# Decayed state on GpSimd, two row-tile homes changed, and wider-spaced weight conversions in a fused attention and expert kernel

## The chip, the cores and the metric

One core of a Trainium2 chip runs the whole program. The metric is device time in microseconds (us). Three runs of the kernel before took 591.41, 592.48 and 594.57 us, so the median is 592.48 us.

## What is computed

The reference has three parts in a row. The first is causal attention with decay: 2 batches, 8 heads, 768 positions, head size 64, and a 64x64 state per head that is decayed and added to from block to block. The second is a dense feed-forward layer on the 1536 tokens that result. The third sends every token to the best of 8 experts.

```python
kv_state = lam_block[None, :, None, None] * kv_state + np.einsum('bhsd,bhse->bhde', kb_dec, vb)
...
h = x @ w_in
g = h * np.tanh(sp)
return (g @ w_out).astype(np.float32)
...
h = np.maximum(x[mask] @ w1[e], 0.0)
out[mask] = gate_w[mask, None] * (h @ w2[e])
```

## The kernel before, in words

**Tiling.** The 1536 tokens are 12 tiles of 128. Attention handles one tile per call of attend (L837), with blocks of 128 positions instead of 64, so six calls make a batch. Three tiles make a chunk of 384 tokens, and there are four chunks. The dense layer has 2048 hidden units in 16 pieces of 128, numbered fc. For a chunk and a piece, mm1 (L791) does twelve matmuls into PSUM and a chain of five ScalarE and five VectorE instructions for the activation. mm2a (L815) does nine matmuls that add the piece to three PSUM accumulators, one per token tile. Every operand is held as a high and a low part, hence three products for each.

**Order of the main loop (L861).** Step i takes one pair (chunk, piece) from a list of 64: chunks 0, 1 and 2 with pieces 0 to 7, then the same chunks with pieces 8 to 15, then chunk 3 with all 16. In a step mm1 works on pair i, and mm2a on pair i-3. There are only three accumulators. After pieces 0 to 7 of a chunk, put_by (L386) copies the three accumulators with ScalarE into row tiles and sends them to memory. Later fetch (L392) loads them back, and route (L410) adds them. So put_by happens in steps 10, 18 and 26 for chunks 0, 1 and 2, and mm2a of the next step needs the accumulators empty. The first fetch stands in step 32. Attention tiles 3 to 11 are done inside steps 0 to 8.

**Weights.** Each of the 32 weight pieces (16 of w_in, 16 of w_out) arrives as 64-bit floats and is converted on the chip. load_wi (L286) and load_wo (L295) take a staging tile (L281), load 512 KB into it on SyncE's queue, and call convert (L269): three ScalarE instructions (L272, L273, L276), two VectorE (L274, L275) and one GpSimd subtraction (L277, shown under the helper's line L102). The staging tile is free again when that subtraction is done. Staging tiles come from a list of tags used in turn. In steps 9 and on the list is `cv, wo14, cv, wo15`, and from the moment that the next conversion is piece 13 of w_in it is `cv, cv`. The tag cv has two buffers; wo14 and wo15 have one each, which hold attention tiles (pms, L137) before, and the converted pieces 14 and 15 of w_out at the end. convert_next (L305) takes the next pieces in order. Half of the 32, those with fc under 8, are converted in the attention steps. In steps from 9 on, L873 asks for 2, 1, 1, 2, 1, 1 and so on.

**Row tiles.** row_tiles (L378) gives put_by, fetch and the last route one cv buffer, which holds two rows of tiles, and the tile xq, which holds the third.

**State.** combine (L193) computes a tile's contribution to the state in PSUM (sp, L203). For the first tile of a batch it is copied (L218). For the next four, VectorE decays the old state and adds sp in one instruction per pair of heads: four instructions of 128x64 (L221). The sixth tile of a batch needs no new state. So there are 32 such instructions. GpSimd in attention scales the keys and the queries (L188, L191, both shown under L102) and does the conversions' subtractions.

**What sets the order on a queue.** Each engine and SyncE's queue runs its instructions in a fixed order. It is made ahead of time, from the place in the program and from when each instruction is reckoned to be ready. So a later conversion can stand ahead of an earlier instruction that is not ready, and a load can stand far ahead of its use.

Of the kernel before, what the change touches and what calls it, by code (L numbers as in the profile page):

```python
# [7 lines left out]
F32 = mybir.dt.float32  # L8
# [5 lines left out]
ALU = mybir.AluOpType  # L14
AX = mybir.AxisListType
P = 128
# [10 lines left out]
FA = 8  # L27
# [4 lines left out]
def tile_decay_attention_mish_moe_top1(  # L32
# [16 lines left out]
    B, H, S, D = q.shape  # L49
    NT, DM = out.shape  # L50
    NE, _, FF = w1.shape
    HP = H // 2
# [13 lines left out]
    def T(shape, dt, tag, bufs=1):  # L66
        return pool.tile(shape, dt, tag=tag, name=tag, bufs=bufs)
# [28 lines left out]
    def PS(shape, tag):  # L96
        return psp.tile(shape, F32, tag=tag, name=tag, bufs=NBUF[tag])

    V, A, G = nc.vector, nc.scalar, nc.gpsimd

    def tt(o, a, b, op, eng=None):
        (eng or V).tensor_tensor(out=o, in0=a, in1=b, op=op)  # L102

    def bc(ap, n):
        return ap.unsqueeze(len(ap.shape)).to_broadcast(list(ap.shape) + [n])
# [32 lines left out]
    sts = T([P, 4, HP, D], F32, "wo13")  # L138
# [8 lines left out]
    def qT(it):  # L147
        return qTs[it // 2 % 2][:, it % 2]
# [44 lines left out]
    def combine(it):  # L193
        b, c = it // CPB, it % CPB
        kd, vt = kd2[:, it % 2], vr2[:, it % 2]
        pm = pms[it % 2]
        qd = qT(it)
        st_old, st_new = sts[:, c % 2], sts[:, (c + 1) % 2]
        if c < CPB - 1:
            sp = PS([P, HP, D], "w" if it < SHARED else "r")  # L200
            for hp in range(HP):
                for r in range(2):
                    nc.tensor.matmul(sp[64 * r:64 * r + 64, hp, :], lhsT=kd[:, 2 * hp + r, :], rhs=vt[:, 2 * hp + r, :],  # L203
                                     start=True, stop=True)
        po = PS([P, HP, P], "a" if it < SHARED else "w")
        for hp in range(HP):
            for r in range(2):
                s = slice(64 * r, 64 * r + 64)
                if c > 0:
                    nc.tensor.matmul(po[s, hp, :], lhsT=st_old[s, hp, :], rhs=qd[s, hp, :], start=(hp == 0), stop=False,  # L210
                                     skip_group_check=True)
        for hp in range(HP):
            for r in range(2):
                s = slice(64 * r, 64 * r + 64)
                nc.tensor.matmul(po[s, hp, :], lhsT=vt[:, 2 * hp + r, :], rhs=pm[:, r, hp, :], start=(c == 0 and hp == 0), stop=True,
                                 skip_group_check=True)
        if c == 0:
            V.tensor_copy(st_new, sp)  # L218
        elif c < CPB - 1:
            for hp in range(HP):  # L220
                V.scalar_tensor_tensor(out=st_new[:, hp], in0=st_old[:, hp], scalar=lc[:, hp:hp + 1], in1=sp[:, hp],  # L221
                                       op0=ALU.mult, op1=ALU.add)
        ck, o = it // CT, (it % CT) * P
        if o == 0:
            xth[ck] = T([P, KC, CW], F32R, f"xth{ck}")
            xtl[ck] = T([P, KC, CW], F32R, f"xtl{ck}")
        A.activation(out=xth[ck][:, :, o:o + P], in_=po, func=AF.Copy)
        tt(xtl[ck][:, :, o:o + P], po, xth[ck][:, :, o:o + P].bitcast(F32), ALU.subtract)
# [31 lines left out]
    lc = tabq[:, :, P - 1]  # L260
# [44 lines left out]
    def convert_next(n, limit=NFC):  # L305
        for _ in range(n):
            ok = [w for w in wq if w[2] < limit]
            if ok:
                wq.remove(ok[0])
                _, kind, f = ok[0]  # L310
                (load_wi if kind == "i" else load_wo)(f)
# [66 lines left out]
    def row_tiles():  # L378
        xa = T([P, 2, DM], F32, "cv", 2)
        xq = T([P, DM], F32, "xq")  # L380
        return [xa[:, 0], xa[:, 1], xq[:, :]]

    def part_rows(c, j):
        return part[(CT * c + j) * P:(CT * c + j + 1) * P, :]

    def put_by(c, acc):  # L386
        rows = row_tiles()
        for j in range(CT):
            A.activation(out=rows[j], in_=acc[j], func=AF.Copy, scale=2.0)  # L389
            nc.sync.dma_start(out=part_rows(c, j), in_=rows[j])  # L390
# [394 lines left out]
    def step():  # L785
        if steps:
            f = steps.pop(0)
            if f is not None:
                f()
# [71 lines left out]
    for i, (c, fc) in enumerate(order):  # L861
        it = CT + i
        if it < NIT:
            if it == NIT - CT:
                stg["tags"] = ["cv", "cv", "wi10"]
            attend(it)
            convert_next(2, FA)
        else:
            if it == NIT:
                stg["tags"] = ["cv", "wo14", "cv", "wo15"]  # L870
            if wq and wq[0][2] >= 13:
                stg["tags"] = ["cv", "cv"]
            convert_next(2 if i < FA + 1 or i % 3 == 0 else 1)  # L873
        mm1(c, fc)
        step()
        if c == NCK - 1:
            early(1, fc)
        if i >= LAG:
            mm2a(*order[i - LAG])
        step()  # L880
# [310 lines left out]
```

## Time and profile before

| | us |
|---|---|
| runs | 591.41, 592.48, 594.57 |
| profiled execution, whole | 593.29 |
| its span, first to last instruction | 591.6 |
| PE busy | 534.8 |
| VectorE busy | 342.3 |
| ScalarE busy | 303.1 |
| GpSimd busy | 114.9 |

The profiled execution is 0.81 us above the median of the runs. 1.7 us of it lie outside the span. Busy time of PE is an upper bound of its work, because matmuls overlap and their ends are modelled. The granted clock of TensorE, 1.00 for 2.4 GHz, tells where the same matmuls ran slower: its other level, 1.2 GHz, is half.

### The profile page before, as it was taken

The page shows a single profiled execution, that of the slowest core. Times are in us where ns is not written, and L with a number is a line of the kernel's source. Part 1 is how long each engine was busy: PE and PEld are TensorE (multiplying, and loading weights), DVE is VectorE, ACT ScalarE, POOL GpSimd, SP SyncE. Part 2 cuts the span into 40 slices and gives each one's busy share as a digit, 9 for nine tenths or more (in the row PEclk, how much of TensorE's full clock was granted, in tenths as well). Part 3 has the DMA queues.
Part 4 walks back from the last instruction along what each step waited for, and adds up shares of the span by engine and source line. Part 5 has one row for each costly group of instructions (what it writes and reads, how often), then busy time and mean ns, then how long its engine had stood idle before and what let it go on. Part 6 is the DMA issues. An engine that isn't in the chain of part 4 may idle for free. (4 is left out here: it accounts for less than half of the span.)

```text
span 591.6 us, 10189 instructions
## 1 busy us (share of the span) xinstructions
PE 534.8 (90%) x3568; PEld 465.9 (79%) x3568; DVE 342.3 (58%) x815; ACT 303.1 (51%) x581; POOL 114.9 (19%) x99
## 2 busy tenths in 40 slices
PE   4899899999879999999999999999889968878990
PEld 2678788888768989899999998898788858667870
DVE  3467898777987765867677699748320233212110
ACT  3257878568888666566565678531221244112110
POOL 1264464422221100000000012001413022030300
PEclk9999999999898999999999999988999998989996
DMA  8669874224343020020030072001696183020300
GB/s 200 154 153 251 204 200 144 81 81 143 107 124 108 18 90 1 0 90 19 0 108 1 27 251 96 2 10 48 202 342 244 38 274 124 10 83 12 93 24 19
DMA packets 67214, 61.76 MB, mean 104 GB/s; under 512 B 42151, under 2 KB 51887, under 8 KB 67120
## 3 DMA queue, kind: packets, MB, share of 16 engines
q1 hardware_dynamic: 64304, 51.70, 29.1%
q0 software_dynamic: 2816, 8.92, 4.9%
q8 instruction: 46, 0.75, 0.6%
q14 instruction: 48, 0.39, 0.2%
HBM read 51.94 MB, written 8.86 MB: 103 GB/s over the span
## 5 line engine op out<-in xcount | busy, mean ns | idle before, releaser
L824 PE MATMUL a<-wo,mg 128*128 128x512 f32 x576 | 149.5, 402 | 5.1 <-ACT xq L389 2.8
L798 PE MATMUL w<-xth,wi 128*128 128x384 f32 x512 | 144.2, 342 | 2.9 <-DVE me L810 2.5
L824 PEld LDWEIGHTS a<-wo,mg 128*128 128x128 f32 x576 | 108.4, 191 | 27.7 <-ACT xq L389 3.8
L798 PEld LDWEIGHTS w<-xth,wi 128*128 128x128 f32 x512 | 93.9, 188 | 7.1 <-DVE me L810 2.9
L576 PE MATMUL w<-wi,wi 128*128 128x256 f32 x576 | 78.1, 295 | 15.3 <-issue 12.0
L576 PEld LDWEIGHTS w<-wi,wi 128*128 128x128 f32 x576 | 74.9, 200 | 18.3 <-issue 13.6
L798 PE MATMUL w<-xtl,wi 128*128 128x384 f32 x256 | 86.3, 337 | 0.0
L580 DVE SCALAR_TENSOR_TENSOR wo<-w,wi 128x256 fp32r<-128x256 f32 x48 | 20.0, 424 | 91.5 <-ACT wi L579 88.3
L566 PE MATMUL a<-wo,wi 128*128 128x512 f32 x192 | 62.8, 409 | 3.7 <-ACTq L1135 2.8
L808 DVE SCALAR_TENSOR_TENSOR me<-me,mg 128x384 f32<-128x384 f32 x64 | 42.2, 659 | 34.7 <-ACT mg L807 34.7
L579 ACT ACTIVATE wi<-w 128x256 fp32r<-128x256 f32 x48 | 18.1, 385 | 66.6 <-PE w L576 65.4
L798 PEld LDWEIGHTS w<-xtl,wi 128*128 128x128 f32 x256 | 48.3, 188 | 1.8
L803 ACT ACTIVATE me<-w 128x384 f32<-128x384 f32 x64 | 31.1, 485 | 30.1 <-PE w L798 29.9
L566 PEld LDWEIGHTS a<-wo,wi 128*128 128x128 f32 x192 | 35.7, 192 | 13.0 <-issue 5.5
L805 ACT ACTIVATE me<-me,one 128x384 f32<-128x384 f32 x64 | 39.2, 612 | 12.6 <-DVE me L804 12.3
L811 ACT ACTIVATE mg<-me 128x384 fp32r<-128x384 f32 x64 | 33.3, 521 | 23.5 <-DVE me L810 23.1
L102 DVE TENSOR_TENSOR mg<-me,mg 128x384 fp32r<-128x384 f32 x64 | 37.5, 586 | 11.9 <-ACT mg L811 11.2
L806 ACT ACTIVATE mr<-me,one 128x384 f32<-128x384 f32 x64 | 39.3, 614 | 1.2
L809 DVE SCALAR_TENSOR_TENSOR me<-me,mg 128x384 f32<-128x384 f32 x64 | 38.3, 599 | 1.0
L566 PE MATMUL a<-wo,wo 128*128 128x512 f32 x96 | 38.5, 402 | 0.0
L810 DVE SCALAR_TENSOR_TENSOR me<-me,w 128x384 f32<-128x384 f32 x64 | 35.2, 550 | 1.2
L807 ACT ACTIVATE mg<-mr 128x384 fp32r<-128x384 f32 x64 | 33.4, 522 | 1.3
(268 smaller groups left out, 699.7 us busy)
## 6 DMA issues: line engine op xcount, KB each, us to landing
xtl<-in_moe_w_dram SPq DMA_DIRECT2D x24, 256.0 KB
cv<-in_moe_w_out_dram SPq DMA_DIRECT2D x11, 512.0 KB
cv<-in_moe_w_in_dram SPq DMA_DIRECT2D x9, 512.0 KB
wi<-in_moe_w_dram SPq DMA_DIRECT2D x8, 512.0 KB
wo<-in_moe_w_dram SPq DMA_DIRECT2D x8, 512.0 KB
wo<-in_k_dram SPq DMA_DIRECT2D x12, 256.0 KB
wi<-in_q_dram SPq DMA_DIRECT2D x12, 256.0 KB
wo<-in_v_dram SPq DMA_DIRECT2D x12, 256.0 KB
```

Source lines behind the costliest of these rows:

```text
L102: (eng or V).tensor_tensor(out=o, in0=a, in1=b, op=op)
L566: nc.tensor.matmul(po, lhsT=a_, rhs=b_, start=(f == 0 and i == 0), stop=(f == FC2 - 1 and i == 2))
L576: nc.tensor.matmul(ph, lhsT=a_, rhs=b_, start=(n == 0), stop=(n == 3 * KC - 1))
L798: nc.tensor.matmul(ph, lhsT=a_, rhs=b_, start=(n == 0), stop=(n == 3 * KC - 1))
L805: A.activation(out=ex, in_=ex, func=AF.Square, bias=one[:, 0:1])
L806: A.activation(out=rr, in_=ex, func=AF.Ln, bias=one[:, 0:1])
L807: A.activation(out=gg[:, 1], in_=rr, func=AF.Exp, scale=-1.0)
L808: V.scalar_tensor_tensor(out=ex, in0=ex, scalar=1.0, in1=gg[:, 1].bitcast(F32), op0=ALU.add, op1=ALU.mult)
L809: V.scalar_tensor_tensor(out=ex, in0=ex, scalar=-2.0, in1=gg[:, 1].bitcast(F32), op0=ALU.add, op1=ALU.mult)
L810: V.scalar_tensor_tensor(out=ex, in0=ex, scalar=0.5, in1=ph, op0=ALU.add, op1=ALU.mult)
L811: A.activation(out=gg[:, 0], in_=ex, func=AF.Copy)
L824: nc.tensor.matmul(accs[c][j], lhsT=a_, rhs=b_, start=(fc in (0, divided_at) and i == 0), stop=(fc in (divided_at - 1, NFC - 1) and i == 2))
```

## The change

Three edits. The state's decay becomes one GpSimd multiplication of 128x256 into a third slice of the state tile, and one VectorE addition of 128x256 takes the place of the four instructions. For chunks 0 and 1, put_by takes its row tiles under the tags wo15 (rows 0 and 1) and wo14 (row 2) instead of cv and xq; chunk 2 and everything later stay with cv and xq. In the main loop the conversions asked for in steps 9 and on become 0, 1, 1, 0, 1, 1 and so on. (The new condition `i <= FA` never holds there, since this branch starts with step 9 and FA is 8.)

```diff
-        st_old, st_new = sts[:, c % 2], sts[:, (c + 1) % 2]
+        st_old, st_new, st_dec = sts[:, c % 2], sts[:, (c + 1) % 2], sts[:, 2]
...
-            for hp in range(HP):
-                V.scalar_tensor_tensor(out=st_new[:, hp], in0=st_old[:, hp], scalar=lc[:, hp:hp + 1], in1=sp[:, hp],
-                                       op0=ALU.mult, op1=ALU.add)
+            tt(st_dec, st_old, bc(lc, D), ALU.mult, G)
+            tt(st_new, sp, st_dec, ALU.add)
...
     def put_by(c, acc):
-        rows = row_tiles()
+        if c < 2:
+            xa = T([P, 2, DM], F32, "wo15")
+            xb = T([P, 2, DM], F32, "wo14")
+            rows = [xa[:, 0], xa[:, 1], xb[:, 0]]
+        else:
+            rows = row_tiles()
...
-            convert_next(2 if i < FA + 1 or i % 3 == 0 else 1)
+            convert_next(2 if i <= FA else 1 if i % 3 else 0)
```

## Rows read from the trace of the kernel before

**Rows 1.** The page's first part: engine, busy us, share of span, instructions.

```profile
PE 534.8 (90%) x3568; PEld 465.9 (79%) x3568; DVE 342.3 (58%) x815; ACT 303.1 (51%) x581; POOL 114.9 (19%) x99
```

**Rows 2.** Busy time by stretch: attention, first pass, second pass, experts.

```profile
core 0: us, PE busy (x) PEld busy (x) DVE busy (x) ACT busy (x) POOL busy (x), PEclk, DMA share, GB/s
...
45.00:121.20 76.20, 72.69 (x662) 60.66 (x658) 65.10 (x114) 57.79 (x108) 36.53 (x26) 1.00 0.65 174
121.20:183.40 62.20, 54.75 (x252) 47.71 (x253) 50.30 (x84) 52.66 (x103) 16.91 (x12) 0.95 0.35 111
183.40:234.00 50.60, 50.60 (x256) 45.71 (x255) 34.27 (x66) 33.34 (x68) 3.24 (x2) 1.00 0.15 52
...
400.00:591.60 191.60, 157.41 (x1169) 135.33 (x1168) 50.99 (x168) 39.98 (x84) 36.12 (x35) 0.94 0.35 116
```

**Rows 3.** PE's waits, 121.2 to 183.4 us: total us, times, longest us.

```profile
PE a L824 <- ACT xq L389: 2.8, 2, 2.4
PE w L798 <- DVE me L810: 2.5, 1, 2.5
```

**Rows 4.** Timeline of PE around the second put_by: start, us, instruction, [idle before].

```profile
166.53 2.22 PE L824 MATMUL a<-wo,mg 128*128 128x512 f32 x9
...
173.22 0.98 PE L824 MATMUL a<-wo,mg 128*128 128x512 f32 x3 [2.35 <-ACT xq L389]
...
178.57 5.07 PE L824 MATMUL a<-wo,mg 128*128 128x512 f32 x14 [2.03 <-ACT cv L389]
```

**Rows 5.** Timeline of ACT: the copies of the second put_by.

```profile
172.57 0.59 ACT L389 ACTIVATE xq<-a 128x512 f32<-128x512 f32 x1
...
177.94 1.06 ACT L389 ACTIVATE cv<-a 128x512 f32<-128x512 f32 x2
```

**Rows 6.** Timeline of SyncE's queue around the second put_by.

```profile
166.50 6.57 SPq L297 DMA_DIRECT2D cv<-in_moe_w_out_dram  x2
...
182.28 0.99 SPq L297 DMA_DIRECT2D cv<-in_moe_w_out_dram  x2
```

**Rows 7.** Busy time by stretch: one step or part, columns as in rows 2.

```profile
150.10:156.00 5.90, 5.82 (x21) 5.21 (x22) 5.68 (x12) 5.90 (x13) 1.86 (x2) 0.71 0.30 100
156.00:160.20 4.20, 4.20 (x22) 3.79 (x21) 3.44 (x6) 2.81 (x6) 1.24 (x1) 1.00 0.57 177
178.50:183.40 4.90, 4.83 (x14) 3.84 (x15) 3.18 (x7) 4.83 (x11) 1.30 (x1) 0.65 0.38 120
216.00:220.00 4.00, 4.00 (x22) 3.62 (x21) 2.47 (x5) 2.51 (x6) 0.00 (x0) 1.00 0.19 66
```

**Rows 8.** Timeline: first ScalarE instruction and GpSimd end of the last conversions.

```profile
186.59 0.68 ACT L272 ACTIVATE cv<-cv 128x512 f32<-128x512 f32 x1
...
190.61 3.24 POOL L102 TENSOR_TENSOR wo<-cv,wo 128x512 fp32r<-128x512 f32 x2 [8.36 <-ACT wo L276]
```

**Rows 9.** Groups by shape, 20 to 121.2 us: count, busy us, mean ns, idle before.

```profile
L221 DVE SCALAR_TENSOR_TENSOR wo<-wo,xq,w 128x64 f32<-128x64 f32 x16 | 3.7, 273 | 1.3 <-PE w L203 1.3
...
L218 DVE COPY wo<-w 128x256 f32<-128x256 f32 x1 | 0.4, 413 | 0.0
...
L102 POOL TENSOR_TENSOR wi<-wi,xq 128x512 f32<-128x512 f32 x10 | 14.0, 1398 | 7.0 <-PE w L177 7.0
L102 POOL TENSOR_TENSOR wi<-wo,wo 128x512 f32<-128x512 f32 x10 | 12.1, 1216 | 3.4 <-DMA wo<-in_k_dram 2.1 <-ACT wo L255 1.3
```

**Rows 10.** PE's waits, 45 to 121.2 us.

```profile
PE w L177 <- DVE xtl L102: 1.0, 2, 0.5
PE r L203 <- POOL wo L102: 0.3, 1, 0.3
```

**Rows 11.** Timelines of VectorE and GpSimd: one instruction alone, then beside GpSimd.

```profile
63.72 0.68 DVE L275 SCALAR_TENSOR_TENSOR cv<-cv 128x512 int32<-128x512 int32 x1
...
65.40 1.80 DVE L275 SCALAR_TENSOR_TENSOR xtl<-xtl 128x512 int32<-128x512 int32 x1
...
65.23 1.42 POOL L102 TENSOR_TENSOR wo<-cv,wo 128x512 fp32r<-128x512 f32 x1 [4.81 <-ACT wo L276]
```

## The prediction

> **What bounds the kernel now.** First the page: PE is busy 90% of the span, no other engine over 58% [rows 1]. So time is to be had only where PE stands still or runs at its lower clock. The table by stretch says where that is [rows 2]. From 183.4 us on, PE is busy for the whole of 50.60 us at a clock of 1.00. The experts at the end hold the largest idle time, 191.60 - 157.41 = 34 us, but no edit reaches them. Attention, from 45 us, leaves 3.5 us idle. The first pass over the dense layer, 121.2 to 183.4 us, is steps 9 to 20 (252 matmuls, 21 in a step): PE is busy for 54.75 of 62.20 us, and the clock is 0.95. That is 7.45 us of idle time, and this stretch has the edits' target in it.
>
> Why does PE wait there? VectorE is busy for 50.30 / 12 = 4.19 us a step, ScalarE for 52.66 / 12 = 4.39 us, and a step of PE takes 4.20 us where nothing disturbs it [rows 2, 7]. So ScalarE has slightly more work than PE, and what PE needs from it comes late. The list of waits names two things [rows 3]: the copies of put_by (L389), and the activation chain (L810), once for 2.5 us. The timeline shows the copies' case. The accumulators of chunk 1 are finished at 168.75 us [rows 4], yet the copy into xq comes at 172.57 us and those into cv at 177.94 us [rows 5]. PE stands idle for 2.35 and for 2.03 us meanwhile [rows 4]. SyncE's queue gives the reason: two weight loads took both cv buffers between 166.50 and 173.07 us, just ahead of put_by, and the next two loads follow it at 182.28 us [rows 6]. The sums wait for a weight conversion to finish with its staging tile.
>
> Behind the two long idle times the clock falls. The stretch from 150.1 us has a granted clock of 0.71, that from 178.5 us 0.65, so part of each ran at 1.2 GHz [rows 7]. The first takes 5.90 us for a step that takes 4.20 us after it: 1.70 us, of which 0.08 idle, so 1.6 us. The second holds 14 matmuls of mm2a in 4.83 us; at the pace of rows 4 (nine in 2.22 us; 0.23 us each from start to start) they take 3.2 us, so 1.6 us more.
>
> **Row tiles.** Chunks 0 and 1 no longer ask for cv or xq. The tiles wo15 and wo14 belonged to attention's scores, read last in step 8, so put_by in step 10 finds them free. In step 18 it finds them free if pieces 11 and 12 of w_in, which are staged there, are converted. Nothing is added: three copies and three stores each, on the same queues. What goes is the second put_by's lateness: 2.35 + 2.03 + 1.6 of clock = 6.0 us. What is late next is the load of piece 9 on wo14, which now stands behind the store of row 2 on SyncE's queue, and the loads behind it; they are needed in step 24 at the earliest, so this is covered. Without that cover each would cost a load.
>
> **Spacing.** After the change two conversions come in three steps. The stretch before the change did 12 in 12 steps (GpSimd's 12 instructions in rows 2). A step without one costs ScalarE 2.51 us and VectorE 2.47 us in 4.00 us [rows 7], so about 2.55 and 2.5 us in a step. A conversion with its share of the copies is then 4.39 - 2.55 = 1.84 and 4.19 - 2.5 = 1.7 us, and two thirds of them give ScalarE 3.8 us and VectorE 3.6 us a step. Both are under PE's 4.20 us. So the wait on L810 should go: 2.5 + 1.6 us of clock = 4.1 us. The remaining 0.6 us of idle time (7.45 - 4.38 - 2.49) I leave where it is, and take it for the lower end.
>
> The conversions are not fewer. They reach into steps 21 to 32, where PE has no idle time, ScalarE is busy for 33.34 and VectorE for 34.27 of 50.60 us [rows 2]; four to eight more at 1.84 us add 7 to 15 us and still fit. The last stands in step 32, near 121.2 + 23 x 4.2 = 217.8 us. The last two took 7.3 us together from the first ScalarE instruction to GpSimd's end [rows 8], so its weights are there by 225.1 us. mm2a needs them in step 34, at 121.2 + 25 x 4.2 + 2.1 = 228.3 us. The cover is 3 us, and if it is gone PE waits for piece 15.
>
> The third put_by (step 26) still uses cv and xq. Before, no conversion ran then; now the two ahead of it hold both cv buffers, as they did at the second put_by. From below it costs nothing, for the conversions may run ahead of their places; from above the 6.0 us of the second put_by. Only half as many are asked for as in step 18, so I take a quarter, 1.5 us.
>
> **State.** Out go 32 VectorE instructions of 0.273 us, 8.7 us in all in two such groups [rows 9]. In come 8 additions of 128x256. The copy of that shape from PSUM took 0.413 us [rows 9], so 3.3 us: VectorE is relieved of 5.4 us by these means, less where four ran back to back. GpSimd gains 8 multiplications of 128x256. Nearest are its 128x512 ones, 1.216 and 1.398 us [rows 9]; half is 0.6 to 0.7, some 5 us in all, on an engine busy 36.53 of 76.20 us [rows 2]. What of it is on the path? PE waited 1.0 us for VectorE's subtraction behind the state, and 0.3 us for GpSimd's keys [rows 10]. So it may gain 1.0 us; it may lose up to 5 us, if each addition waits for GpSimd and holds up the subtraction, and with it the next step, by a whole multiplication. The state is needed only one tile later, so I take 0.
>
> There is contention. VectorE's L275 takes 0.68 us alone, and 1.80 us when it starts at 65.40 us, while a GpSimd instruction runs from 65.23 to 66.65 us; it ends 0.55 us after that one, as if it had waited for its end [rows 11]. So each new multiplication can hold up such an instruction by its own 0.6 to 0.7 us, which gives back most of VectorE's 5.4 us.
>
> The Trainium skill's page "SBUF — State Buffer", section "SBUF: two separate sides", says that VectorE instructions with two SBUF inputs and GpSimd instructions exclude each other for a whole instruction. The trace agrees, with the 1.80 us. The rule speaks against this edit: by it VectorE gets little, its 1.0 us of waits stay, and the sum is the 584.7 us below; if the two engines did not exclude each other, the 1.0 us would go, and the sum would be 583.7 us.
>
> **Sum.** Against the profiled execution's own 593.29 us, which is 0.81 us above the median of the runs: 593.29 - 6.0 - 4.1 + 1.5 = 584.7 us. With nothing lost at the third put_by, with the 0.6 us and the 1.0 us, it is 581.6 us. With its full 6.0 us it is 589.2 us, and with 3 us lost in attention beside that 592.2 us.
>
> **Rivals.** (1) *The wait moves to the third put_by.* The pattern is the same: two conversions just ahead in the queue, two buffers. For it speaks that cv is now the only staging tag from then on; against it that conversions have room to run ahead. It gives back 6.0 us: 589.2 us.
>
> (2) *Spacing does nothing.* Loads stand far ahead of their use, so conversions can crowd as before, whatever the loop asks. Then only the row tiles pay, 593.29 - 6.0 = 587.3 us. Against it: a lower place in the program makes them yield to the copies and the activation chain.
>
> (3) *GpSimd's decay holds up attention* by its upper end, 5 us: 589.7 us. Against it is the tile of slack.
>
> (4) *Slower: the weight loads get wo14 and wo15 first.* Those loads wait for nothing but the tile, while put_by waits for the sums. Pieces 9 and 11 would then sit in them, with their conversions behind put_by in the program: piece 11 stands in step 14, three steps after PE needs the accumulators, 3 x 4.2 = 12.6 us. At the second put_by the same happens with pieces 11 and 12, or not. One such wait costs up to 12.6 us and, with 10.1 us gained, turns the sum to 595.8 us; two make 608 us. It decides once the waits exceed 10.1 us. Against it: at the second put_by the loads ahead in the program went first and those behind it came after, at 182.28 us [rows 6], as in program order.
>
> **How the numbers follow.** A measurement here can tell about 0.5% from no change: under 589.5 us is faster, over 595.4 us slower. The forecast (581 to 588 us) gets 0.58; rival 1 gets 0.13, spread around 589.2 us, half of it faster; rival 2 gets 0.11, faster; rival 3 gets 0.06, half of it faster; rival 4 gets 0.12, of which 0.09 slower and the rest within. Faster: 0.58 + 0.065 + 0.11 + 0.03, rounded down to 0.77 for an unnamed wait. Same: 0.14. Slower: 0.09. The range runs from 580.5 us, a little under the 581.6 us, to 592 us, the end with both losses; it leaves out rival 4 and some of the tails, under 2 in 10.
>
> **What would show it.** Right: steps 9 to 20 take about 12 x 4.2 = 50.4 us without idle time over 1 us or a clock under 1.00; the copies of the first two put_by write wo tiles within 2 us of the sums; GpSimd's last subtraction comes after 205 us. The 32 rows of L221 are gone, 8 multiplications of 0.6 to 0.7 us are new, and attention's 76.20 us stay within 1 us. Wrong: PE waiting for L389 near 205 us (rival 1) or 131 us (rival 4), for a converted w_out piece after 215 us, or a step before 121.2 us that grew.

## The result, and the profile after

The changed kernel takes 599.28 us (median of four runs, 598.24 to 601.92) where the kernel before takes 592.58 us in the same comparison. The ratio is 1.012, with a 95% interval of 1.0082 to 1.0157: it is slower. The forecast was 584.7 us with a range of 580.5 to 592, so both the time and the sign were wrong. The profiled execution after took 601.92 us, which is 2.64 us above the median; its span is 600.2 us, 8.6 us more than before.

After the change mm1's matmul is L802, mm2a's L828, put_by's copy L393 and its store L394. The activation chain is L807 to L815, and its last VectorE instruction, which PE waits for, is L814 (L810 before). A conversion is L271 to L276, and route's addition is L426. In the experiments that have the row-tile edit without the state edit, all of these are one line further on: L394, L427, L803, L815, L829.

The page's first part answers to [rows 1]:

```profile
PE 536.9 (89%) x3568; PEld 466.9 (78%) x3568; DVE 344.8 (57%) x791; ACT 302.4 (50%) x581; POOL 120.5 (20%) x107
```

VectorE has 24 instructions fewer and GpSimd 8 more, as the state edit says. The first surprise is that VectorE's busy time did not fall by 5.4 us: it rose by 2.5 us.

The next view is the table by stretch, cut at the starts of mm1 in steps 0, 9, 21, 35, 37 and 63, first of the kernel after, then of the kernel before at its own starts (columns as in [rows 2]):

```profile
42.98:128.01 85.03, 75.72 (x661) 63.71 (x659) 70.19 (x102) 60.05 (x112) 40.23 (x31) 0.94 0.58 157
128.01:186.40 58.39, 53.74 (x254) 46.45 (x252) 45.76 (x77) 44.95 (x92) 13.86 (x9) 0.97 0.32 105
186.40:245.30 58.90, 58.84 (x296) 52.96 (x295) 40.58 (x75) 42.12 (x83) 5.86 (x4) 1.00 0.16 54
245.30:259.50 14.20, 12.53 (x64) 10.84 (x62) 10.61 (x21) 8.84 (x17) 0.00 (x0) 0.88 0.00 0
259.50:381.79 122.29, 122.29 (x670) 111.12 (x668) 93.69 (x240) 80.89 (x151) 5.76 (x3) 1.00 0.20 72
```

```profile
45.11:121.21 76.10, 72.58 (x660) 60.66 (x658) 65.11 (x114) 57.79 (x108) 36.53 (x26) 1.00 0.65 174
121.21:183.48 62.27, 54.83 (x253) 47.75 (x253) 50.38 (x84) 52.73 (x103) 16.91 (x12) 0.95 0.35 111
183.48:242.09 58.61, 58.61 (x296) 52.95 (x294) 39.17 (x76) 38.41 (x78) 3.24 (x2) 1.00 0.13 45
242.09:252.50 10.41, 10.41 (x64) 9.58 (x62) 8.50 (x17) 6.99 (x14) 0.00 (x0) 1.00 0.00 1
252.50:374.79 122.29, 122.29 (x670) 111.14 (x669) 93.92 (x240) 81.71 (x152) 5.76 (x3) 1.00 0.21 72
```

Line against line, attention (steps 0 to 8) grew by 8.9 us, the first pass (steps 9 to 20) shrank by 3.9, steps 21 to 34 grew by 0.3, steps 35 and 36 grew by 3.8, and the steps from 37 to 62 are equal. The start came 2.1 us earlier and what follows step 63 took 1.6 us more; kernels with nothing edited in these two places differ by as much (below). So the loss is attention's, and the gain of the first pass was given back by step 37.

**Attention.** PE's waits from 45 to 128 us, which answer to [rows 10]:

```profile
PE w L210 <- DVE wo L102: 3.8, 2, 2.1
PE r L203 <- issue: 1.9, 1, 1.9
PE w L215 <- DVE wo L102: 1.7, 1, 1.7
PE w L802 <- DVE wo L102: 1.0, 1, 1.0
PE w L177 <- DVE me L814: 0.9, 1, 0.9
```

The waits add up to 9.3 us, and most name VectorE's writing of `wo` from PSUM (L102 `wo<-w,wo`), which are attention's masked scores. None names GpSimd. In the kernel before, PE stood idle for 3.5 us, and the longest wait, which [rows 10] leave out, was for ScalarE:

```profile
PE r L203 <- ACT wi L168: 1.4, 1, 1.4
```

Of the growth of 8.9 us, 5.8 us are idle time of PE (9.31 - 3.52) and 3.1 us are longer busy time (75.72 - 72.58), at a granted clock of 0.94 instead of 1.00.

Why are the scores late? Here are VectorE and then GpSimd after the change, in step 2, around the place of [rows 11], and the wait of PE that follows:

```profile
64.61 1.78 DVE L274 SCALAR_TENSOR_TENSOR xtl<-xtl 128x512 int32<-128x512 int32 x1
66.31 1.45 DVE L808 TENSOR_SCALAR me<-me 128x384 f32<-128x384 f32 x1
67.68 1.27 DVE L102 TENSOR_TENSOR wo<-w,wo 128x512 f32<-128x512 f32 x2
```

```profile
64.37 1.47 POOL L102 TENSOR_TENSOR wi<-wi,xq 128x512 f32<-128x512 f32 x1 [5.54 <-ACT wo L275]
65.80 1.75 POOL L102 TENSOR_TENSOR wo<-cv,wo 128x512 fp32r<-128x512 f32 x1
```

```profile
68.42 0.76 PE L215 MATMUL w<-wo,wo 128*64 128x128 f32 x9 [1.73 <-DVE wo L102]
```

Two VectorE instructions in a row, of 0.68 and 0.35 us alone, take 1.78 and 1.45 us, each beside GpSimd work; the scores stand behind them in VectorE's fixed order, and PE behind the scores. The GpSimd instructions of 1.47 and 1.75 us are not new, only in another order: in the kernel before, `wo<-cv,wo` came first. None of GpSimd's new multiplications stands in this place: the next one starts at 70.92 us. The kernel in which VectorE does the multiplication (f1, below) gives GpSimd nothing new and has the same rows here, VectorE's and then GpSimd's (its L803 is L808 after the change):

```profile
64.20 1.78 DVE L274 SCALAR_TENSOR_TENSOR xtl<-xtl 128x512 int32<-128x512 int32 x1
65.91 1.45 DVE L803 TENSOR_SCALAR me<-me 128x384 f32<-128x384 f32 x1
```

```profile
63.97 1.46 POOL L102 TENSOR_TENSOR wi<-wi,xq 128x512 f32<-128x512 f32 x1 [5.58 <-ACT wo L275]
65.39 1.75 POOL L102 TENSOR_TENSOR wo<-cv,wo 128x512 fp32r<-128x512 f32 x1
```

Step 2 takes 11.8 us there, 11.7 us after the change and 8.7 us before. So this place comes from the new order that the split of the decay brought, and not from GpSimd's added work. In that kernel PE worked through step 2 at a clock of 0.86 and was busy for 10.8 us; after the change it worked at 1.00, was busy for 9.1 us and waited. The step is as long either way: here the lower clock fills time in which PE would have waited, so idle time and longer busy time are not separate costs.

In step 3 the same happens once more, and this time not in the kernel where VectorE multiplies:

```profile
75.11 1.77 DVE L274 SCALAR_TENSOR_TENSOR wi<-wi 128x512 int32<-128x512 int32 x1
76.80 1.45 DVE L808 TENSOR_SCALAR me<-me 128x384 f32<-128x384 f32 x1
```

```profile
78.91 0.86 PE L210 MATMUL w<-wi,wo 64*64 64x128 f32 x10 [1.73 <-DVE wo L102]
```

The step takes 13.2 us after the change, 11.9 and 13.4 us in the other two kernels whose addition reads GpSimd's product (e1 and f3, below), and 10.6 to 10.7 us before and in f1.

**First pass.** The idle times at the second copies, 2.35 and 2.03 us before [rows 4], shrank to 1.50 us in step 19 (those at the first are 0.17 and 0.94 us in step 11, where it was 0.43 us), and the granted clock rose from 0.95 to 0.97. But in place of the wait of 2.5 us on the activation chain in step 15 there is one of 2.01 us in step 16, at 161.87 us, with a clock of 0.71 behind it. SyncE's queue shows what comes before it, and GpSimd and VectorE the rest:

```profile
138.79 3.12 SPq L394 DMA_DIRECT2D part<-wo  x3
...
144.36 11.83 SPq L287 DMA_DIRECT2D wo<-in_moe_w_in_dram  x3
```

```profile
154.00 1.80 POOL L102 TENSOR_TENSOR wi<-wo,wi 128x512 fp32r<-128x512 f32 x1 [10.09 <-ACT wi L275]
155.75 1.77 POOL L102 TENSOR_TENSOR wi<-cv,wi 128x512 fp32r<-128x512 f32 x1
157.48 1.62 POOL L102 TENSOR_TENSOR wi<-wo,wi 128x512 fp32r<-128x512 f32 x1
159.06 1.61 POOL L102 TENSOR_TENSOR wo<-cv,wo 128x512 fp32r<-128x512 f32 x1
```

```profile
156.27 1.67 DVE L102 TENSOR_TENSOR mg<-me,mg 128x384 fp32r<-128x384 f32 x1
157.86 1.66 DVE L812 SCALAR_TENSOR_TENSOR me<-me,mg 128x384 f32<-128x384 f32 x1
159.55 1.53 DVE L813 SCALAR_TENSOR_TENSOR me<-me,mg 128x384 f32<-128x384 f32 x1
...
161.28 0.54 DVE L814 SCALAR_TENSOR_TENSOR me<-me,w 128x384 f32<-128x384 f32 x1
```

The loads into wo14 and wo15 stand behind the first stores. GpSimd's order begins with the subtraction of such a piece, so it stands idle for 10.09 us and then does four subtractions without a gap. Three chain instructions of some 0.56 us take 1.53 to 1.67 us beside them.

**Steps 35 and 36.** PE waits 1.63 us for route's addition, of which VectorE's timeline shows the place:

```profile
249.18 3.23 PE L828 MATMUL a<-wo,mg 128*128 128x512 f32 x9 [1.63 <-DVE cv L426]
```

```profile
247.61 0.55 DVE L814 SCALAR_TENSOR_TENSOR me<-me,w 128x384 f32<-128x384 f32 x1
248.08 0.35 DVE L808 TENSOR_SCALAR me<-me 128x384 f32<-128x384 f32 x1
248.35 0.68 DVE L426 SCALAR_TENSOR_TENSOR cv<-a,cv 128x512 f32<-128x512 f32 x1
```

The sums are ready near 245.4 us, when PE has gone on to the next mm1, but in VectorE's order the addition stands behind the next step's activation chain. Behind the wait nine matmuls take 3.23 us instead of 2.2, and the clock of the stretch is 0.88.

### The profile page after: what moved, and what is told of

Same layout as the page of the kernel before. It is cut to its first block, busy times and chain, and to the rows that moved or that the text cites. A ratio compares the mean times of both kernels' runs of the same rounds, so it can differ in the third digit from the quotient of the medians.

```text
span 600.2 us, 10182 instructions
## 1 busy us (share of the span) xinstructions
PE 536.9 (89%) x3568; PEld 466.9 (78%) x3568; DVE 344.8 (57%) x791; ACT 302.4 (50%) x581; POOL 120.5 (20%) x107
## 4 chain that ended last, share of the span: by engine, by line
PE 38%; issue 23%; DMA 15%; DVE 10%; ACT 8%; POOL 3%; POOLq 1%; SPq 0%; DVEq 0%; ACTq 0%
PE a L828 12%; PE w L802 12%; DMA xth<-x2d,xth 5%; DMA out_dram<-cv,xth 5%; PE w L580 2%; PE w L177 2%; DMA cv<-in_moe_w_out_dram 2%; DVE me L808 2%; PE r L440 2%; ACT me L809 1%; DVE me L812 1%; ACT mr L810 1%; DVE me L813 1%; DVE mg L102 1%; PE r L433 1%
## 5 line engine op out<-in xcount | busy, mean ns | idle before, releaser
L828 PE MATMUL a<-wo,mg 128*128 128x512 f32 x576 | 148.7, 399 | 4.3 <-ACT wo L393 2.6
L802 PE MATMUL w<-xth,wi 128*128 128x384 f32 x512 | 145.6, 345 | 3.1 <-DVE me L814 2.0
L828 PEld LDWEIGHTS a<-wo,mg 128*128 128x128 f32 x576 | 106.7, 189 | 27.2 <-ACT wo L393 4.5
L802 PEld LDWEIGHTS w<-xth,wi 128*128 128x128 f32 x512 | 95.0, 190 | 8.1 <-DVE me L814 3.4
L580 PEld LDWEIGHTS w<-wi,wi 128*128 128x128 f32 x576 | 75.5, 202 | 17.9 <-issue 12.9
L802 PE MATMUL w<-xtl,wi 128*128 128x384 f32 x256 | 86.9, 339 | 0.0
L812 DVE SCALAR_TENSOR_TENSOR me<-me,mg 128x384 f32<-128x384 f32 x64 | 39.7, 620 | 31.2 <-ACT mg L811 30.9
L802 PEld LDWEIGHTS w<-xtl,wi 128*128 128x128 f32 x256 | 49.0, 191 | 1.7
L102 DVE TENSOR_TENSOR mg<-me,mg 128x384 fp32r<-128x384 f32 x64 | 38.2, 597 | 18.2 <-ACT mg L815 17.6
L807 ACT ACTIVATE me<-w 128x384 f32<-128x384 f32 x64 | 31.2, 487 | 33.3 <-PE w L802 32.9
L815 ACT ACTIVATE mg<-me 128x384 fp32r<-128x384 f32 x64 | 33.2, 519 | 18.3 <-DVE me L814 17.8
L810 ACT ACTIVATE mr<-me,one 128x384 f32<-128x384 f32 x64 | 39.2, 612 | 1.1
L813 DVE SCALAR_TENSOR_TENSOR me<-me,mg 128x384 f32<-128x384 f32 x64 | 38.3, 599 | 1.2
L570 PE MATMUL a<-wo,wo 128*128 128x512 f32 x96 | 37.9, 395 | 0.0
L814 DVE SCALAR_TENSOR_TENSOR me<-me,w 128x384 f32<-128x384 f32 x64 | 35.2, 550 | 1.1
L808 DVE TENSOR_SCALAR me<-me 128x384 f32<-128x384 f32 x64 | 31.8, 498 | 5.2 <-ACT me L807 4.6
```

The costliest lines, as they stand in the source:

```text
L570: nc.tensor.matmul(po, lhsT=a_, rhs=b_, start=(f == 0 and i == 0), stop=(f == FC2 - 1 and i == 2))
L580: nc.tensor.matmul(ph, lhsT=a_, rhs=b_, start=(n == 0), stop=(n == 3 * KC - 1))
L802: nc.tensor.matmul(ph, lhsT=a_, rhs=b_, start=(n == 0), stop=(n == 3 * KC - 1))
L808: V.tensor_scalar(out=ex, in0=ex, scalar1=EXP20, scalar2=None, op0=ALU.min)
L810: A.activation(out=rr, in_=ex, func=AF.Ln, bias=one[:, 0:1])
L812: V.scalar_tensor_tensor(out=ex, in0=ex, scalar=1.0, in1=gg[:, 1].bitcast(F32), op0=ALU.add, op1=ALU.mult)
```

## The experiments

All ratios are to the kernel before on the same chip. The tables further down cut each profiled execution at the starts of mm1. They are one execution each; the kernel before, profiled once more, shows how far such numbers scatter (590.06 us; nothing edited):

> The kernel before unchanged, for a second profile of it: how far do two profiles of one program differ, and where? If attention and the two passes repeat: every step starts within 0.3 us of the first profile, and what differs in the time lies behind step 63. If not, differences of steps under that scatter carry nothing.

Its step 0 starts 1.7 us earlier, steps 0 to 8 take 75.7 us against 76.1, steps 9 to 20 take 60.1 against 62.3, and steps 9 to 36 take 130.2 against 131.3. Every engine runs its instructions in the same order in both profiles. So differences under some 2 us within the first pass say nothing, and against this second profile the first pass gained only 1.7 us by the change. The best gauge of attention are steps 2 to 7: the ten profiles without an edit in attention or in the weights that it converts (these two and eight below) take 54.8 to 54.9 us for them, and 75.5 to 77.2 us for steps 0 to 8. Where nothing was edited, step 0 starts between 42.9 and 45.2 us, and what follows step 63 takes between 214.2 and 218.9 us.

### One edit at a time

State edit alone:

```diff
-                V.scalar_tensor_tensor(out=st_new[:, hp], in0=st_old[:, hp], scalar=lc[:, hp:hp + 1], in1=sp[:, hp],
+            tt(st_dec, st_old, bc(lc, D), ALU.mult, G)
+            tt(st_new, sp, st_dec, ALU.add)
```

> Only the decay edit, the rest as before. Theory D (the decay on GpSimd makes attention longer, the other two edits help): the first activation of step 9 comes 5 to 9 us later than the 125.2 us of before, and the time is 597 to 602 us. Theory S (the loss comes from the conversions' and row tiles' new places, which also rearrange attention, and the decay is neutral): step 9 within 1.5 us of before, time 591 to 594 us.

Measured: 598.49 us, ratio 1.0135 [1.0073, 1.0197]. This edit alone loses as much as the three together.

Row tiles and spacing without it:

```diff
+        if c < 2:
+            xa = T([P, 2, DM], F32, "wo15")
+            xb = T([P, 2, DM], F32, "wo14")
...
+            convert_next(2 if i <= FA else 1 if i % 3 else 0)
```

> The change without its decay edit: row tiles and spacing together. Theory D: attention as before (step 9 near 125 us), the first pass free of long waits, time 584 to 590 us, faster than both kernels. Theory S: step 9 is 5 to 9 us late as in the changed kernel, time 597 to 601 us.

Measured: 594.37 us, 1.0045 [1.0013, 1.0078]. The two edits meant for the first pass gain nothing together; theory D's 584 to 590 us did not come.

Row tiles alone:

```diff
+        if c < 2:
+            xa = T([P, 2, DM], F32, "wo15")
+            xb = T([P, 2, DM], F32, "wo14")
```

> Only the row tiles. Theory D with the prediction's own term: the second put_by's lateness goes, 6.0 us less, 585 to 589 us. Theory S: the row tiles wait for or hold up weight loads, time 592 us or more.

Measured: 593.75 us, 1.0036 [1.0007, 1.0066]. From 121 to 260 us PE waits three times for the chain, 4.5 us in all, and 2.9 us for the copies. The kernel before waited 2.5 us for the chain and 4.8 us for the copies (2.8 us for xq [rows 3] and 2.0 us for cv [rows 4]). So the copies' wait did shrink, and the chain's grew by as much.

Spacing alone:

```diff
-            convert_next(2 if i < FA + 1 or i % 3 == 0 else 1)
+            convert_next(2 if i <= FA else 1 if i % 3 else 0)
```

> Only the wider spacing. Theory D with the prediction's own term: the wait on the activation chain near 150 us goes, about 4 us less, and the second put_by's wait for cv gets shorter too: 584 to 590 us. Theory S: attention or the second pass grows, time 594 us or more.

Measured: 590.2 us, 0.9975 [0.9943, 1.0008], no difference that can be told. But the trace shows 9.7 us gained in steps 9 to 20 (7.5 us against the second profile) and 8 us lost after them. Its stretches around the loss (from step 9 to the start of step 21, then to 200 us, then to 210 us) and the waits in it:

```profile
120.61:173.14 52.53, 51.32 (x253) 45.28 (x252) 37.82 (x66) 39.33 (x79) 6.89 (x6) 1.00 0.23 81
173.14:200.00 26.86, 25.77 (x127) 22.42 (x125) 24.63 (x38) 21.67 (x42) 8.71 (x6) 1.00 0.24 78
200.00:210.00 10.00, 6.67 (x25) 5.17 (x26) 5.98 (x13) 8.29 (x18) 0.00 (x0) 0.87 0.42 139
```

```profile
200.69 0.45 PE L798 MATMUL w<-xth,wi 128*128 128x384 f32 x1 [1.12 <-DVE me L810]
...
205.66 3.54 PE L824 MATMUL a<-wo,mg 128*128 128x512 f32 x9 [2.62 <-ACT cv L389]
```

The first pass was freed of its long waits: of the 4.4 us at the second copies of sums, which still use cv and xq, 1.06 us are left. But GpSimd began only five conversions in these steps, where the kernel before had begun twelve. The other eleven come later, and PE then stands at the third copies.

### What the state edit costs, and through what

The same split with VectorE multiplying:

```diff
-            tt(st_dec, st_old, bc(lc, D), ALU.mult, G)
+            tt(st_dec, st_old, bc(lc, D), ALU.mult)
```

> The decay edit alone, but its multiplication on VectorE instead of GpSimd, so the wide addition stays and GpSimd gets nothing. Theory G (GpSimd's extra work is the cost, through the two engines' mutual exclusion): step 8 starts within 2 us of the 116.4 us of before, time 589 to 595 us. Theory O (one wide addition in place of four narrow instructions rearranges the queues, whoever multiplies): step 8 near 122.5 us as with the decay on GpSimd, time 596 to 601 us.

Measured: 591.72 us, 1.0011 [0.9977, 1.0046]. In the whole time the two VectorE instructions in place of four cost nothing that can be told. In attention they do: steps 2 to 7 take 60.2 us, 5.4 us more than before, with nothing added on GpSimd. Step 8 started at 118.1 us, within theory G's 2 us, only because step 0 had started 2.6 us early. Up to step 37 the cost is gone: steps 0 to 1 are 1.0 us shorter and steps 9 to 36 take 128.6 us, so steps 0 to 36 take 208.5 us, inside the 205.9 to 209.5 us of the ten profiles named above.

The three runs f2, h1 and i1 add GpSimd multiplications into slices of the state tile that nothing reads. First, eight of them beside the kernel before:

```diff
+            tt(sts[:, 2], st_old, bc(lc, D), ALU.mult, G)
             for hp in range(HP):
```

> The kernel before with the eight GpSimd multiplications added and their result read by nobody; the four VectorE instructions stay. Theory G: VectorE's two-input instructions are stretched as in the changed kernel (12 us in steps 2 to 8 against 8.5 us), step 8 is 4 to 8 us late, time 596 to 602 us. Theory O, and a theory that the wait for the decayed state is what costs: time 591 to 594 us.

Measured: 593.41 us, 1.0026 [0.9994, 1.0059]. Theory G's 596 to 602 us did not come: added GpSimd work alone does not make the loss either.

The product made one tile earlier, so that the addition never waits for it:

```diff
+            tt(st_new, sp, sts[:, 2 + c % 2], ALU.add)
+        if c < CPB - 2:
+            tt(sts[:, 2 + (c + 1) % 2], st_new, bc(lc, D), ALU.mult, G)
```

> The decay edit alone, with GpSimd's multiplication placed right behind the state that it decays, one tile earlier in the program. If what costs is the place on GpSimd's queue (the decay stands late and VectorE's addition with the work behind it waits): step 8 within 2 us of before, 589 to 594 us. Theory G: the same eight multiplications exclude VectorE as long wherever they stand, 596 to 601 us.

Measured: 598.0 us, 1.0121 [1.008, 1.0162], as with the edit itself. So it is no wait of the addition for its product.

Sixteen unread multiplications:

```diff
+            tt(sts[:, 2], st_old, bc(lc, D), ALU.mult, G)
+            tt(sts[:, 3], st_old, bc(lc, D), ALU.mult, G)
```

> The kernel before with sixteen unread GpSimd multiplications instead of eight. Theory G: the stretch of VectorE's two-input instructions in steps 2 to 8 grows again, from 10.7 to 13 to 15 us, and step 8 is 7 to 10 us late against 4.5 us with eight. If the eight were late by a chance of the order: step 8 is 2 to 6 us late, with no growth.

Measured once: 594.45 us, 4.7 us over its chip's median for the kernel before, where eight cost 2.6 us; one run cannot tell these apart. In its profile attention is no longer than with eight (table below).

VectorE's split, with the unread multiplication beside it:

```diff
+            tt(st_dec, st_old, bc(lc, D), ALU.mult)
+            tt(sts[:, 3], st_old, bc(lc, D), ALU.mult, G)
```

> The split decay with its multiplication on VectorE, as in the run that did that alone (1.001), and beside it the same multiplication on GpSimd into a slice of the state tile that nothing reads. Theory W (what costs is where the two engines meet: some TensorE waits of 2 us for the masks, and the lower clock behind them, and they need GpSimd to be busy at the wrong moment, whoever reads its result): some 3 to 8 us over the kernel before, ratio 1.005 to 1.013, and at least three waits over 1 us between 45 and 125 us. Theory D (it takes a reader: VectorE's addition waits for GpSimd's product, or is placed differently for it): within 2 us of the run without the unread multiplication, ratio 0.997 to 1.005, and one or two waits over 1 us.

Measured: 596.46 us, 1.0128 [1.0099, 1.0158]. Nothing reads GpSimd's product, and the loss is there in full. So it takes no reader; it takes the split and GpSimd's multiplications together, for either alone cost nothing clear of the noise. PE's longest waits from 45 to 128 us in this run:

```profile
PE w L210 <- DVE wo L102: 2.6, 1, 2.6
PE w L177 <- DVE xtl L102: 2.5, 3, 1.5
PE w L215 <- DVE wo L102: 1.7, 1, 1.7
```

These and the two shorter ones are waits for VectorE, like nearly all after the change. The kernels of this group side by side, steps 0 to 8 of each profiled execution, and the lengths of two other stretches, us:

| kernel | steps 0 to 8 | PE idle | PE busy | clock | GpSimd busy | steps 2 to 7 | steps 0 to 36 |
|---|---|---|---|---|---|---|---|
| before | 76.1 | 3.52 | 72.58 | 1.00 | 36.5 | 54.8 | 207.4 |
| before, profiled again | 75.7 | 3.25 | 72.43 | 1.00 | 36.5 | 54.8 | 205.9 |
| decay on VectorE | 79.9 | 5.94 | 73.95 | 0.98 | 37.1 | 60.2 | 208.5 |
| 8 unread | 80.2 | 6.40 | 73.85 | 0.98 | 37.9 | 58.6 | 210.5 |
| 16 unread | 78.7 | 5.04 | 73.67 | 0.98 | 42.8 | 58.0 | 208.6 |
| decay on VectorE, 8 unread | 81.5 | 9.17 | 72.35 | 1.00 | 40.4 | 61.9 | 210.7 |
| state edit alone | 83.6 | 9.04 | 74.56 | 0.96 | 40.7 | 64.0 | 213.1 |
| product one tile earlier | 84.4 | 9.94 | 74.45 | 0.96 | 40.6 | 64.8 | 213.9 |
| after | 85.0 | 9.31 | 75.72 | 0.94 | 40.2 | 65.4 | 216.5 |

The four kernels with the split and GpSimd work have 9 to 10 us of idle time, the others 3 to 6.4. Those with a clock under 1.00 were busy for 1 to 3 us longer. The length does not follow GpSimd's busy time (the sixteen unread have the most). What the rows shown above suggest is that it follows where the engines meet, which shifts when the fixed order does; no run changes the order alone, so this is not shown for every step. Why the split is hurt more by the multiplications than the four old instructions is not settled. Nor is how much of the loss lies outside attention: between the two kernels with the decay on VectorE, the unread multiplications made 2.2 us up to step 37, while the medians, each against its own chip's, lie 6 us apart. (The run with 8 unread is 4.8 us above its median in its profile, so its row is an unfavourable one.)

### Where the first pass's gain goes

Spacing, with the wo tiles for the third copies only:

```diff
+        if c == 2:
+            xa = T([P, 2, DM], F32, "wo15")
+            xb = T([P, 2, DM], F32, "wo14")
```

> Spacing as in the change, no decay edit, and the tiles wo15 and wo14 given to the third put_by instead of the first two. With spacing alone 10 us were won by step 21, and 7 us lost again at steps 24 to 28, where the third put_by waited for cv. If that wait is what gives the gain back: step 28 starts 8 to 10 us ahead of before and the time is 581 to 586 us, faster than both kernels. If the conversions' work itself comes due there: 588 to 592 us.

Measured: 591.78 us, 1.0024 [1.0, 1.0048]. PE's waits from 160 to 260 us:

```profile
PE a L829 <- ACT wo L394: 5.2, 1, 5.2
PE a L829 <- ACT cv L394: 1.1, 1, 1.1
```

The third copies were late all the same, by more, in tiles of their own. So the wait was not for cv. PE had done its last matmul before it by 200.0 us; ScalarE shows what stood ahead of the copies:

```profile
202.11 0.68 ACT L272 ACTIVATE cv<-cv 128x512 f32<-128x512 f32 x1 [0.67 <-DMA cv<-in_moe_w_out_dram]
...
204.52 0.59 ACT L394 ACTIVATE wo<-a 128x512 f32<-128x512 f32 x1
```

In ScalarE's order they come behind instructions of the activation chain and of two conversions, one of which waited 0.67 us for its load.

Spacing, wo tiles for the second and third copies:

```diff
+        if c >= 1:
+            xa = T([P, 2, DM], F32, "wo15")
+            xb = T([P, 2, DM], F32, "wo14")
```

> Spacing, no decay edit, wo15 and wo14 for the second and third put_by; only the first keeps cv and xq. With spacing alone GpSimd did no conversion between 145 and 173 us, because the later ones come after the second put_by in the turn for cv. If that turn is what crowds the conversions into steps 21 to 32 and the third put_by's copies behind them: GpSimd works on through 145 to 173 us, the third put_by waits under 1 us, step 28 starts 8 us or more ahead of before, time 580 to 587 us. If ScalarE's fixed order holds the copies up anyway: a wait of 2 to 5 us at step 27 again, 588 to 592 us.

Measured: 590.84 us, 1.0021 [0.9991, 1.0051]. The third copies still cost a wait of 1.3 us, and the second, now in wo tiles, 2.8 us; the gain of 8 us or more by step 28 did not come.

Spacing, wo tiles for the second copies only:

```diff
+        if c == 1:
+            xa = T([P, 2, DM], F32, "wo15")
+            xb = T([P, 2, DM], F32, "wo14")
```

> As the last, but only the second put_by uses wo15 and wo14. With spacing and both early put_by on them, 1.4 us were lost at step 12 and 3.3 us at steps 17 to 20, behind the loads of pieces 9, 11 and 12 that stood behind the first put_by's stores. If that is the cost of the row tiles: neither loss here, step 21 at least 8 us ahead of before. What is lost at the third put_by stays: time 586 to 591 us. If the loss has another cause: step 21 within 5 us of before, 592 us or more.

Measured: 589.56 us, 1.0000 [0.9969, 1.0031]. Without the first put_by in wo tiles step 11 loses 0.2 us instead of 1.9 us (after the change), but steps 9 to 20 gained 5.2 us and not the 8 us expected: four waits for the chain (1.7 us) and three at the second copies (3.1 us) are left. The wait for route's addition (1.6 us) is there as after the change.

One conversion in each step, so that the last is asked for two steps ahead of the third copies:

```diff
-            convert_next(2 if i < FA + 1 or i % 3 == 0 else 1)
+            convert_next(1)
```

> The kernel before with one conversion asked for in every step from 9 on, so that the sixteen are asked for by step 24, two steps ahead of the third copies of sums. Theory T (the wider spacing takes the waits out of the first pass, and its gain is lost at the third copies only since conversions then still surround them): some 5 to 9 us gained by step 20, of which at least 4 us still stand at step 37, ratio 0.985 to 0.993. Rival B (the work of the engines other than TensorE is a backlog that has to be done before step 37, so that what is gained early is lost wherever the copies come): gain at step 37 under 2 us whatever was gained before, ratio 0.996 to 1.002.

Measured: 593.16 us, 1.0043 [1.0016, 1.0071]. PE now waits seven times, 7.0 us in all, for the activation chain.

The same with the second copies in wo tiles:

```diff
+            convert_next(1)
...
+        if c == 1:
```

> The same with the second copies of sums in the wo tiles. Theory T: as the run with one conversion in a step or up to 3 us better, since the idle times of the second copies go (2.35 and 2.03 us before), ratio 0.98 to 0.992. Rival B: as before, ratio 0.996 to 1.004, the start of step 37 within 2 us of the kernel before.

Measured: 590.19 us, 1.0013 [0.9985, 1.0042]. As rival B said: PE still waits 2.4 us for the chain in step 18, 2.2 us at the second copies and 1.9 us at the third.

No conversions from step 9 on:

```diff
                 stg["tags"] = ["cv", "wo14", "cv", "wo15"]
+                wq.clear()
+                for f in range(FA, NFC):
+                    wi[f], wo[f] = wi[f - FA], wo[f - FA]
```

> The kernel before with the sixteen conversions of steps 9 and on left out, loads included: pieces 8 to 15 of the dense layer use the converted weights of pieces 0 to 7 in their place. Theory C (the gain of the first pass is given back since the conversions, wherever they are put before step 37, make the copies of sums or the activation chain late at some place): without them steps 9 to 37 take near 29 x 4.2 us and little more, 120 to 124 us where they take 129 to 130 us in nearly all kernels so far; 6 to 10 us less at step 37, ratio 0.982 to 0.991. Rival K (the copies, the fetches and route's additions alone hold TensorE up, conversions or not): 127 us or more from step 9 to step 37, ratio 0.994 to 1.002.

Measured: 595.27 us, 1.008 [1.0044, 1.0116]. The time is no answer: with other weights the tokens go to other experts, and what follows step 63 takes 234.6 instead of 216.8 us. That this is the routing was not tried. The steps up to 63 are the answer. Steps 9 to 20, 21 to 34, and 35 and 36:

```profile
120.75:170.98 50.23, 50.23 (x254) 45.57 (x252) 30.35 (x60) 33.70 (x66) 0.00 (x0) 1.00 0.10 37
170.98:229.51 58.53, 58.53 (x296) 53.10 (x295) 36.30 (x73) 38.68 (x74) 0.00 (x0) 1.00 0.07 23
229.51:239.96 10.45, 10.45 (x64) 9.62 (x62) 7.68 (x16) 6.15 (x12) 0.00 (x0) 1.00 0.00 0
```

PE has no idle time at all, with the copies, the fetches and route's additions in place. All kernels of this group, us from one start of mm1 to another, and the conversions whose GpSimd subtraction began in steps 9 to 20:

| kernel | conversions | steps 9 to 20 | 21 to 36 | 9 to 36 |
|---|---|---|---|---|
| before | 12 | 62.3 | 69.0 | 131.3 |
| before, profiled again | 12 | 60.1 | 70.1 | 130.2 |
| after | 9 | 58.4 | 73.1 | 131.5 |
| row tiles and spacing | 9 | 59.5 | 71.9 | 131.5 |
| row tiles | 11 | 59.3 | 73.0 | 132.3 |
| spacing | 5 | 52.5 | 77.3 | 129.9 |
| spacing, third on wo | 5 | 52.5 | 78.0 | 130.5 |
| spacing, second and third on wo | 9 | 58.5 | 71.6 | 130.1 |
| spacing, second on wo | 9 | 57.0 | 75.4 | 132.4 |
| one in each step | 9 | 57.5 | 74.6 | 132.1 |
| one in each step, second on wo | 9 | 57.0 | 73.0 | 130.0 |
| no conversions | 0 | 50.2 | 69.0 | 119.2 |

Up to ten us change hands between the two stretches, and the sum stays within 129.9 to 132.4 us until the conversions go. The first pass is short where few conversions fall into it: its gain is in large part work put off. So theory C of the last run holds for the steps, if not for the time: the sixteen conversions, loads included, cost 11 to 13 us in every place that was tried. Neither ScalarE nor VectorE is full (39.33 and 37.82 of 52.53 us in the spacing run), so this is no matter of total work; in each kernel another named wait of the fixed orders takes the place of the one removed. Why the sums come out so nearly equal is open. None of these versions beats the kernel before by more than the noise.

## Why the prediction was wrong

Two steps failed: the state's term of 0, which turned the sign, and the 8.6 us booked for the other two edits (-6.0 - 4.1 + 1.5), of which nothing was left at step 37.

**State decay, taken as 0.** Steps 0 to 8 took 7.5 us more with this edit alone (6.8 us of the whole time) and 8.9 us more after, in a stretch that was to stay "within 1 us" of 76.20. Three things in the term were wrong. First, the path was drawn through the state's addition, which has a tile of slack. The slack is there, as the product made one tile earlier shows (1.0121). But the path that counted goes over the masked scores, which share VectorE's order. Second, the bound from above was 5 us, the sum of eight new multiplications (they took 6.7 us): it counted what the new instructions could hold up by their own length. But the edit, VectorE's half of it included, also gives the queues another order, in which old GpSimd instructions of 1.4 to 1.75 us meet VectorE instructions that stand ahead of the scores, and each of these loses up to 1.1 us. With the multiplication left on VectorE that is 5.4 us in steps 2 to 7, and 9.1 us with it on GpSimd. Third, the clock: the first pass's idle times were charged with 1.6 us each, but no such price was set on an idle time of 2 us in attention, where PE was busy for 3.1 us longer. Rival 3 named the place and had a chance of 0.06 and too low a price. What is not settled is why the 5.4 us of the split alone are made good by step 37 and those of the whole edit are not.

The rule drawn from the Trainium skill's page "SBUF — State Buffer", section "SBUF: two separate sides", that VectorE instructions with two SBUF inputs and GpSimd instructions exclude each other, pointed the right way, and every stretched row above with two SBUF inputs agrees with it. The prediction spent it on VectorE's 5.4 us of relief alone. The same section also lists VectorE instructions in a 2-port perf mode as barred; this case's rows show one with a single input, L808, at 1.45 us instead of 0.35, and no run here shows its mode.

**Row tiles, -6.0.** The mechanism was right in part: the copies write wo tiles, and the stores go ahead of the loads, so rival 4 did not happen. But the copies did not come "within 2 us of the sums": the last began 4.4 us after them at the first put_by and 4.6 us at the second, behind other instructions in ScalarE's order. PE's wait for the copies fell from 4.8 to 2.9 us with this edit alone. And "what is late next", the loads into wo14 and wo15, was taken as covered. They are not needed until step 24, but GpSimd's order puts their subtractions ahead of others, and the pile of four cost 2.01 us and a clock of 0.71. Alone the edit measured 1.0036 [1.0007, 1.0066], no gain.

**Spacing, -4.1, and the third put_by, +1.5.** Alone, spacing gained 9.7 us in steps 9 to 20, more than twice the term, and steps of 52.5 / 12 = 4.4 us come near the 4.2 us that were named. But that was not the pace of two conversions in three steps: five were begun where eight were asked for. (The 2.51 and 2.47 us in 4.00 us make 2.6 us in a step of 4.20, not 2.55 and 2.5; the two sums become 3.8 and 3.7 us and stay under 4.20.) At the third put_by it gave back not 1.5 us but some 6 us (its lead over the kernel before, counted from step 9, fell from 9.2 us at step 24 to 3.2 us at step 28), as rival 1 said; but rival 1's reason, the cv buffers, is wrong, since wo tiles there changed nothing (5.2 us of wait). After the change itself the third put_by lost nothing, and the loss came at route's addition instead, which the prediction did not look at because PE had no idle time there before.

**The sum.** 593.29 - 10.1 + 1.5 became, in the span, 591.6 - 2.1 (start) + 8.9 (attention) + 0.2 (steps 9 to 36) + 1.6 (after step 63) = 600.2 us; the start and the last term lie within what kernels with nothing edited there differ by. That 50.4 us are possible in steps 9 to 20 is shown by the kernel without conversions (50.2 us); the prediction took the removal of the two longest waits for the removal of what made them.

## What to carry to other kernels

An edit in a stretch where VectorE is over 80% busy, and an instruction moved to GpSimd above all, is priced by what it does to the order in which the two engines meet, not by the length of its instructions; count the path behind every VectorE instruction that can be held up, clock included. A wait removed in front of fixed in-order queues is a gain only if the next work on the same queues has slack through to the next place where the engines must meet; cost the same work at that place before booking the gain. Compare the running sum at a step after the last edited place, not the stretch that was edited.

## What the runs showed of the hardware that was not expected

A VectorE instruction with one SBUF input, L808 of 128x384, took 1.45 us beside GpSimd and 0.35 us alone. Sixteen unread GpSimd multiplications of 0.755 us on average lengthened steps 2 to 7 by 3.2 us, and eight of 0.679 us by 3.7 us. The split of the decay on VectorE, with nothing new on GpSimd, lengthened them by 5.4 us, and eight unread multiplications of 0.897 us beside it by 1.7 us more. The two profiles of the same program differ by 1.7 us at the first step and by 2.2 us in the first pass, but by under 0.1 us over steps 2 to 7.
